# A two-layer GELU block on one core: both layers in 64-row halves of the matmul array, with another start and another end

## The chip, the core and the metric

The kernel runs on one core of a Trainium2 chip. The metric is the device time of one execution in microseconds, the median of several runs. A profile gives the same execution's span, from its first instruction to its last, and what each engine did in it: TensorE (PE, with its weight loads as PEld), VectorE (DVE), ScalarE (ACT), GpSimd (POOL) and SyncE (SP, which here only issues transfers).

## The reference

```python
# x: 1 x 2048 x 448, w1: 448 x 1792, w2: 1792 x 448, all bf16
def reference(x, w1, b1, w2, b2):
    h = jnp.einsum("bsd,df->bsf", x, w1) + b1
    h = jax.nn.gelu(h, approximate=True)
    return jnp.einsum("bsf,fd->bsd", h, w2) + b2
```

The inner size of layer 1 is 448 = 3 x 128 + 64, so three and a half times the 128 rows of the matmul array. That of layer 2 is 1792 = 14 x 128.

## The kernel before

The 2048 tokens are worked on in four blocks of 512 (`c`). Within a block the 14 tiles of 128 features come in four groups of 4, 4, 4 and 2. For each group layer 1 is done (features on the partitions, 512 tokens as columns), then its GELU, then the group's share of layer 2 (tokens on the partitions, 448 columns), which adds up in four PSUM banks `acc` over the groups. The first block's x is turned on TensorE at the start; the other three are turned by transfers (`transpose=True`).

The start: four tiles of 128 tokens, each turned in four blocks of 128 features. The fourth holds the last 64 features twice, so that both halves of the array can read them.

```python
warm(NWARM)                                     # 5 matmuls of 512 columns on ones
for t in range(STC):
    pr.op("vector", ... xr[:, t, :] <- xn[:, t, D3:D] twice ..., event=("xr", t))
    for k in range(KT + 1):                     # KT = 3
        src = xn[:, t, k * P:(k + 1) * P] if k < KT else xr[:, t, :]
        pr.op("tensor", ... e.transpose(stage(t)[...], src, ident), ...)
    eng = "scalar" if t in (1, 3) else "vector"
    pr.op(eng, evac, after=[("xt", t)], event=("xT0", t))     # 128 x 512 from PSUM
    # [b1 is turned here for t == 1]
warm(NFILL)                                     # 2 more
```

Layer 1 of a group: first the last 64 rows of the inner size, two feature tiles at a time in the two halves of the array, then three matmuls of 128 rows for each tile. Line numbers of the profile stand beside them.

```python
for j in range(n):
    for lo in (0, 1):
        rows = slice(lo * H, (lo + 1) * H)      # H = 64
        pr.op("tensor", ... e.matmul(bank[ft], lhsT=w1r[rows, 2 * gi + j, :],
              rhs=xT[rows, KT, c0:c1], start=True, stop=False))              # L205
for ft in fts:
    for k in range(KT):
        pr.op("tensor", ... e.matmul(bank[ft], lhsT=w1_sb[:, k, ft * P:(ft + 1) * P],
              rhs=xT[:, k, c0:c1], start=False, stop=k == KT - 1))           # L211
    pr.op("scalar", ... GELU of bank[ft] into g, bias b1 ...)                # L216
```

Layer 2, for each feature tile of the group and each of the four token tiles; after the last feature tile VectorE adds b2, and SyncE stores:

```python
pr.op("tensor", ... e.matmul(acc[st][:, 0:D], lhsT=g[:, ft, j * P:(j + 1) * P],
      rhs=w2_sb[:, ft, :], start=ft == 0, stop=fin))                         # L229
if fin:
    pr.op("vector", ... out_sb = acc[st] + b2_bc ...)                        # L233
    pr.dma("sync", ... out <- out_sb[:, j, :] ...)
```

The first group of the first block is done in two halves of 256 tokens. In the last block layer 2 of the last groups is ordered so that the four token tiles end one after the other.

Of the kernel before, what the change touches and what calls it, by code (L numbers as in the profile page):

```python
# [8 lines left out]
FP32 = mybir.dt.float32  # L9


class Program:

# [5 lines left out]
    def __init__(self, nc, es):  # L21
        self.nc, self.es = nc, es
        self.lists = {e: [] for e in self.COMPUTE + ("sync",)}
        self.sems = {e: es.enter_context(nc.semaphore(f"sem_{e}")) for e in self.COMPUTE}
        self.count = dict.fromkeys(self.COMPUTE, 0)
        self.where = {}

    def op(self, engine, make, after=(), event=None):
        if event is not None:
            self.count[engine] += 1  # L30
            self.where[event] = (f"sem_{engine}", self.sems[engine], self.count[engine])
        self.lists[engine].append((make, tuple(after), self.sems[engine] if event else None, 1))

    def dma(self, engine, make, event, after=()):
        if event not in self.where:
            name = "dma_" + "_".join(str(p) for p in (event if isinstance(event, tuple) else (event,)))
            self.where[event] = (name, self.es.enter_context(self.nc.semaphore(name)), 0)
        name, sem, n = self.where[event]
        self.where[event] = (name, sem, n + 16)
        self.lists[engine].append((make, tuple(after), sem, 16))  # L40

    def barrier(self, engine, after):
        self.lists[engine].append((None, tuple(after), None, 0))

    def emit(self, block):
        for name in self.lists:
            getattr(block, name)(lambda eng, name=name: self._run(eng, name))

    def _run(self, eng, name):
        seen = {}  # L50
        for make, after, sem, inc in self.lists[name]:
            for event in after:
                key, s, value = self.where[event]
                if seen.get(key, 0) < value:
                    eng.wait_ge(s, value)
                    seen[key] = value
            if make is None:
                continue
            done = make(eng)
            if sem is not None:  # L60
                done.then_inc(sem, inc)


def bass_standalone__dense_activation_gelu__prompt_kernel(
# [10 lines left out]
    P = 128  # L75
    H = P // 2
    SC = 512
    assert B == 1 and S % SC == 0 and F == 14 * P and D == 3 * P + H
    x2, out2 = x[0], out[0]
    NSC, NST, STC, NFT = S // SC, S // P, SC // P, F // P  # L80
    KT = 3
    D3 = KT * P
    GROUPS = [(0, 1, 2, 3), (4, 5, 6, 7), (8, 9, 10, 11), (12, 13)]
    GC = 4 * P
    NWARM = 5
    NFILL = 2

    with ExitStack() as es:
        sb = lambda name, shape, dt: es.enter_context(nc.sbuf_tensor(name, shape, dt))
        xT = sb("xT", [P, KT + 1, S], BF16)  # L90
        w1_sb = sb("w1_sb", [P, KT, F], BF16)
        w1r = sb("w1r", [P, NFT // 2, P], BF16)
        w2_sb = sb("w2_sb", [P, NFT, D], BF16)
        xn = sb("xn", [P, STC, D], BF16)
        xr = sb("xr", [P, STC, P], BF16)
        ident = sb("ident", [P, P], BF16)
        junk = sb("junk", [P, 1], BF16)
        b1n = sb("b1n", [NFT, P], BF16)
        b1_f = sb("b1_f", [P, NFT], FP32)
        b2_bc = sb("b2_bc", [P, D], BF16)  # L100
        g = sb("g", [P, NFT, S], BF16)
        out_sb = sb("out_sb", [P, NST, D], BF16)
        ps = [es.enter_context(nc.psum_tensor(f"ps_{i}", [P, SC], FP32)) for i in range(4)]
        acc = [es.enter_context(nc.psum_tensor(f"acc_{i}", [P, SC], FP32)) for i in range(4)]

# [4 lines left out]

        x0v = x2[0:SC, :].rearrange("(p t) d -> p t d", t=STC)
        o0v = out2[0:SC, :].rearrange("(p t) d -> p t d", t=STC)

        def group_of(ft):
            return min(ft // 4, len(GROUPS) - 1)


        for a in (0, 2):
            pr.dma("sync", lambda e, a=a: e.dma_start(xn[:, a:a + 2, :], x0v[:, a:a + 2, :]), ("x", a))
        pr.dma("scalar", lambda e: e.dma_start(b1n[:, :], b1.rearrange("(c p) -> c p", p=P)), "b1n")  # L120

        def load_w1(k):
            c0, c1 = k * GC, min((k + 1) * GC, F)
            pr.dma("sync", lambda e: e.dma_start(
                w1_sb[:, :, c0:c1], w1[0:D3, c0:c1].rearrange("(k p) f -> p k f", p=P)), ("w1", k))
            half = (c1 - c0) // 2
            for lo in (0, 1):
                pr.dma("sync", lambda e, lo=lo: e.dma_start(
                    w1r[lo * H:(lo + 1) * H, 2 * k:2 * k + half // P, :],
                    w1[D3:D, c0 + lo * half:c0 + (lo + 1) * half].rearrange("d (j q) -> d j q", q=P)), ("w1", k))  # L130

        def load_w2(k):
            a, b = GROUPS[k][0], GROUPS[k][-1] + 1
            pr.dma("sync", lambda e: e.dma_start(
                w2_sb[:, a:b, :], w2[a * P:b * P, :].rearrange("(f p) d -> p f d", p=P)), ("w2", k))

        for k in range(len(GROUPS)):
            load_w1(k)
            load_w2(k)
        pr.dma("sync", lambda e: e.dma_start(b2_bc[:, :], b2.partition_broadcast(P)), "b2")  # L140
        for c in range(1, NSC):
            for slot, d0 in enumerate((0, P, 2 * P, D - P)):
                pr.dma("sync", lambda e, c=c, slot=slot, d0=d0: e.dma_start(
                    xT[:, slot, c * SC:(c + 1) * SC], x2[c * SC:(c + 1) * SC, d0:d0 + P], transpose=True), ("xT", c))
# [6 lines left out]
        pr.op("scalar", lambda e: e.activation(junk[:, :], one, ACT.Gelu_apprx_tanh))  # L151

        def warm(n):
            for _ in range(n):
                pr.op("tensor", lambda e: e.matmul(ps[1][:, :], lhsT=ones_w, rhs=ones_m, start=True, stop=True))  # L155

        def stage(t):
            return acc[t][:, 0:2 * P].bitcast(BF16)

        warm(NWARM)  # L160
        for t in range(STC):
            a = t - t % 2
            pr.op("vector", lambda e, t=t: e.tensor_copy(  # L163
                xr[:, t, :].rearrange("p (two h) -> p two h", two=2),
                xn[:, t, D3:D].unsqueeze(1).broadcast_to([P, 2, H])), after=[("x", a)], event=("xr", t))
            for k in range(KT + 1):
                src = xn[:, t, k * P:(k + 1) * P] if k < KT else xr[:, t, :]
                need = ["ident", ("x", a)] if k < KT else [("xr", t)]
                pr.op("tensor", lambda e, t=t, k=k, src=src: e.transpose(  # L169
                    stage(t)[:, k * P:(k + 1) * P], src, ident[:, :]),  # L170
                    after=need, event=("xt", t) if k == KT else None)
            eng = "scalar" if t in (1, 3) else "vector"

            def evac(e, t=t, eng=eng):
                o = xT[:, :, t * P:(t + 1) * P]
                i = stage(t).rearrange("p (k s) -> p k s", k=KT + 1)
                return e.copy(o, i) if eng == "scalar" else e.tensor_copy(o, i)  # L177

            pr.op(eng, evac, after=[("xt", t)], event=("xT0", t))
            if t == 1:  # L180
                pr.op("tensor", lambda e: e.matmul(  # L181
                    ps[3][:, 0:NFT], lhsT=b1n[:, :], rhs=ident[0:NFT, 0:NFT], start=True, stop=True),
                    after=["b1n"], event="b1T")
                pr.op("scalar", lambda e: e.copy(b1_f[:, :], ps[3][:, 0:NFT]), after=["b1T"], event="b1")
        warm(NFILL)


        owner = {3: "b1"}

        def layer1(c, gi, cols, last_cols, first_cols):  # L190
            fts = GROUPS[gi]
            n = len(fts) // 2
            c0, c1 = cols
            need = [("w1", gi)] if c == 0 else [("xT", c), ("xTd", c)]
            if c == 0:
                need += [("xT0", t) for t in range(c0 // P, c1 // P)]
            bank = {ft: ps[i] for i, ft in enumerate(fts)}
            for j in range(n):
                for lo in (0, 1):
                    ft = fts[j + lo * n]  # L200
                    rows = slice(lo * H, (lo + 1) * H)
                    after = list(need)
                    if first_cols and fts.index(ft) in owner:
                        after.append(owner[fts.index(ft)])
                    pr.op("tensor", lambda e, ft=ft, rows=rows, j=j: e.matmul(  # L205
                        bank[ft][:, c0 % SC:(c1 - 1) % SC + 1], lhsT=w1r[rows, 2 * gi + j, :],
                        rhs=xT[rows, KT, c0:c1], start=True, stop=False), after=after)
            for ft in fts:
                for k in range(KT):
                    fin = k == KT - 1  # L210
                    pr.op("tensor", lambda e, ft=ft, k=k, fin=fin: e.matmul(  # L211
                        bank[ft][:, c0 % SC:(c1 - 1) % SC + 1], lhsT=w1_sb[:, k, ft * P:(ft + 1) * P],
# [85 lines left out]
```

## Time and profile before

| | |
|---|---|
| time, median of 3 runs | 102.3 us |
| lowest and highest | 100.4 and 102.47 us |
| span of the profile | 101.4 us |
| TensorE busy | 96.2 us, 488 matmuls |
| ScalarE busy | 39.4 us |
| VectorE busy | 11.4 us |
| moved by transfers | 7.27 MB |
| first layer-1 matmul | 7.48 us |

A row of the page's groups reads: line, engine, operation, result <- operands, rows x columns of the array for TensorE, shape, count, then busy time and mean length of one, then how long the engine stood idle just before them and what ended that. The length of one matmul is its whole passage, fill and drain included; since several are under way at once, the pace is seen from when they start. The chain of work that ended last lists, in order of time, what released what, back from the last instruction: start, length and piece.

### The profile page before, as it was taken

How to read it: one execution, taken by the hardware profiler on the slowest of the kernel's cores; microseconds unless marked ns; L12 is line 12 of the kernel's file. 1: busy time of each engine (PE TensorE's matmuls, PEld its weight loads, DVE VectorE, ACT ScalarE, POOL GpSimd, SP SyncE). 2: the span in 40 equal slices, each digit the busy share in tenths (PEclk: the TensorE clock that was granted, in tenths of full speed). 3: DMA queues.
4: the chain of work that ended last, by engine and by line, in shares of the span. 5: the costliest groups of instructions: out<-in, count | busy, mean ns of one | idle time of the engine just before them, and what ended most of it. 6: DMA issues, size and time to landing. Idle time of an engine off the chain costs nothing.

```text
span 101.4 us, 1157 instructions
## 1 busy us (share of the span) xinstructions
PE 96.2 (95%) x488; PEld 42.7 (42%) x488; DVE 11.4 (11%) x25; ACT 39.4 (39%) x61; POOL 0.7 (1%) x6
## 2 busy tenths in 40 slices
PE   6689999999999999999999999999999999999990
PEld 2345553434533443534433444534433534533530
DVE  0320000100006300000008100000008000000081
ACT  4140362807231814609050906419052707238300
POOL 2000000000000000000000000000000000000000
DMA  2999989854430500000001400000002200000023
GB/s 64 275 321 333 343 187 150 75 108 92 95 79 4 177 0 0 6 0 0 0 0 48 133 0 0 0 6 3 0 0 91 91 0 0 0 0 6 0 71 110
DMA packets 13393, 7.27 MB, mean 72 GB/s; under 512 B 7244, under 2 KB 13388, under 8 KB 13388
## 3 DMA queue, kind: packets, MB, share of 16 engines
q1 hardware_dynamic: 13360, 7.20, 27.5%
q8 instruction: 4, 0.07, 0.2%
q14 instruction: 1, 0.01, 0.0%
q10 hardware_dynamic: 28, 0.00, 0.0%
HBM read 3.79 MB, written 1.84 MB: 55 GB/s over the span
## 4 chain that ended last, share of the span: by engine, by line
PE 90%; DMA 3%; ACT 2%; DVE 2%; issue 1%
PE acc L229 42%; PE ps L211 37%; PE ps L205 8%; DMA xn<-in_x_dram 3%; ACT g L216 2%; PE acc L169 2%; PE ps L155 1%; DVE xT L177 1%; DVE out_sb L233 1%; DVE xr L163 0%; PE ps L181 0%
## 5 line engine op out<-in xcount | busy, mean ns | idle before, releaser
L216 ACT ACTIVATE g<-ps,b_f 128x512 bf16<-128x512 f32 x56 | 36.7, 688 | 50.8 <-PE ps L211 50.8
L229 PE MATMUL acc<-w_sb,g 128*128 128x448 bf16 x224 | 44.9, 353 | 0.4
L211 PE MATMUL ps<-xT,w_sb 128*128 128x512 bf16 (+1 forms) x180 | 40.6, 376 | 0.0
L229 PEld LDWEIGHTS acc<-w_sb,g 128*128 128x128 bf16 x224 | 21.6, 98 | 22.3 <-ACT g L216 2.3
L211 PEld LDWEIGHTS ps<-xT,w_sb 128*128 128x128 bf16 x180 | 16.8, 101 | 22.0 <-issue 6.4
L233 DVE TENSOR_TENSOR out_sb<-acc,b_bc 128x448 bf16<-128x448 f32 x16 | 9.2, 618 | 69.4 <-PE acc L229 69.0
L205 PE MATMUL ps<-xT,w1r 64*128 64x512 bf16 (+1 forms) x60 | 9.4, 385 | 0.0
L205 PEld LDWEIGHTS ps<-xT,w1r 64*128 64x128 bf16 x60 | 1.9, 95 | 6.9 <-issue 6.9
L155 PE MATMUL ps<-const-bfloat16-1.0 128*128 128x512 bf16 x7 | 3.4, 627 | 0.8 <-PEq L283 0.8
L177 ACT COPY xT<-acc 128x512 bf16<-128x512 bf16 x2 | 1.2, 586 | 3.2 <-PE acc L169 3.2
L254 DVE COPY xT<-xT 64x512 bf16<-64x512 bf16 x3 | 0.9, 289 | 13.5 <-DMA xT<-in_x_dram 13.4
L169 PE MATMUL acc<-ident,xn 128*128 128x128 bf16 x12 | 1.8, 308 | 0.6 <-DMA xn<-in_x_dram 0.6
L151 ACT ACT_TABLE_LOAD x1 | 1.3, 1283 | 1.4 <-PEq L283 1.4
L169 PEld LDWEIGHTS acc<-ident,xn 128*128 128x128 bf16 x12 | 1.2, 136 | 1.5 <-issue 1.4
L169 PE MATMUL acc<-ident,xr 128*128 128x128 bf16 x4 | 1.2, 302 | 0.6 <-DVE xr L163 0.6
L155 PEld LDWEIGHTS ps<-const-bfloat16-1.0 128*128 128x128 bf16 x7 | 0.8, 133 | 1.6 <-issue 1.6
L163 DVE COPY xr<-xn 128x128 bf16<-128x128 bf16 x4 | 0.7, 188 | 3.5 <-DMA xn<-in_x_dram 3.5
L177 DVE COPY xT<-acc 128x512 bf16<-128x512 bf16 x2 | 0.8, 424 | 1.5 <-PE acc L169 1.5
L169 PEld LDWEIGHTS acc<-ident,xr 128*128 128x128 bf16 x4 | 0.5, 128 | 1.1 <-DVE xr L163 1.1
L148 POOL TENSOR_SCALAR_AFFINE_SELECT ident<-ident 128x128 bf16<-128x128 bf16 x1 | 0.3, 294 | 0.2 <-POOL ident L147 0.2
L151 ACT ACTIVATE junk<-const-bfloat16-1.0 128x1 bf16<-128x1 bf16 x1 | 0.2, 205 | 0.0
L147 POOL MEMSET ident<- 128x128 bf16 x1 | 0.2, 205 | 0.3 <-POOLq L283 0.3
(7 smaller groups left out, 0.9 us busy)
## 6 DMA issues: line engine op xcount, KB each, us to landing
out_dram<-out_sb SPq DMA_DIRECT2D x16, 112.0 KB, 1.7
w_sb<-in_w_dram SPq DMA_DIRECT2D x3, 448.0 KB, 6.1
w_sb<-in_w_dram SPq DMA_DIRECT2D x3, 384.0 KB, 4.2
xn<-in_x_dram SPq DMA_DIRECT2D x2, 224.0 KB, 2.8
w_sb<-in_w_dram SPq DMA_DIRECT2D x1, 224.0 KB, 4.6
w1r<-in_w_dram SPq DMA_DIRECT2D x6, 32.0 KB, 4.3
w_sb<-in_w_dram SPq DMA_DIRECT2D x1, 192.0 KB, 4.5
xT<-in_x_dram SPq DMA_TRANSPOSE x12, 3.6
```

The lines of the kernel that those rows point to most:

```text
L148: pr.op("gpsimd", lambda e: e.affine_select(out=ident[:, :], in_=ident[:, :], compare_op=ALU.not_equal, fill=1.0, base=0, pattern=[[-1, P] ...
L151: pr.op("scalar", lambda e: e.activation(junk[:, :], one, ACT.Gelu_apprx_tanh))
L155: pr.op("tensor", lambda e: e.matmul(ps[1][:, :], lhsT=ones_w, rhs=ones_m, start=True, stop=True))
L163: pr.op("vector", lambda e, t=t: e.tensor_copy(xr[:, t, :].rearrange("p (two h) -> p two h", two=2), xn[:, t, D3:D].unsqueeze(1).broadcast ...
L169: pr.op("tensor", lambda e, t=t, k=k, src=src: e.transpose(stage(t)[:, k * P:(k + 1) * P], src, ident[:, :]), after=need, event=("xt", t) ...
L177: return e.copy(o, i) if eng == "scalar" else e.tensor_copy(o, i)
L205: pr.op("tensor", lambda e, ft=ft, rows=rows, j=j: e.matmul(bank[ft][:, c0 % SC:(c1 - 1) % SC + 1], lhsT=w1r[rows, 2 * gi + j, :], rhs=xT[ ...
L211: pr.op("tensor", lambda e, ft=ft, k=k, fin=fin: e.matmul(bank[ft][:, c0 % SC:(c1 - 1) % SC + 1], lhsT=w1_sb[:, k, ft * P:(ft + 1) * P], r ...
L216: pr.op("scalar", lambda e, ft=ft: e.activation(g[:, ft, c * SC:(c + 1) * SC], bank[ft][:, :], ACT.Gelu_apprx_tanh, bias=b1_f[:, ft:ft + 1 ...
L229: pr.op("tensor", lambda e: e.matmul(acc[st][:, 0:D], lhsT=g[:, ft, j * P:(j + 1) * P], rhs=w2_sb[:, ft, :], start=ft == 0, stop=fin), aft ...
L233: pr.op("vector", lambda e: e.tensor_tensor(out=out_sb[:, j, :], in0=acc[st][:, 0:D], in1=b2_bc[:, :], op=ALU.add), after=[("y", c, st), " ...
L254: pr.op("vector", lambda e, cs=cs: e.tensor_copy(xT[0:H, KT, cs], xT[H:P, KT, cs]), after=[("xT", c + 1)], event=("xTd", c + 1))
```

## The change

What it does:

- **Layer 1 and layer 2 wholly in 64-row halves.** Every matmul of 128 rows becomes two of 64 rows, "a" and "b". Two tiles share a unit of two PSUM banks: in part "a" the first tile uses the upper half of the array and the second the lower, in part "b" the other way round. So the two halves always work on different banks at the same time, and the array is never switched between 128-row and 64-row tiles. Between "a" and "b" of one unit lies other work, and a wait on TensorE's own semaphore keeps both halves from one bank.
- **Order.** Layer 1 of all 14 feature tiles of a block comes first (part "a" of a pair, then part "b" of the pair before), then layer 2 of the block, two token tiles to a unit. The grouping by four goes.
- **The start.** x of the first block comes in one load. SyncE's other loads wait until GpSimd has filled a buffer `b2_z` with zeros; only the first two parts of w1 are issued earlier, on ScalarE's queue. x is turned in halves of 64 tokens side by side: the transposes of rows 0 to 63 and 64 to 127 go to two banks. VectorE moves the result as 32-bit words. Layer 1 begins with the first 256 tokens. The last 64 features are turned later, behind the first matmuls. b1 is turned on VectorE. Seven and a half warming matmuls instead of five, and none after the transposes.
- **The end.** In the last block the last two token tiles are finished side by side in two steps of columns: 0 to 319 in one unit and 320 to 447 in another. b2 is brought into the second tile's bank by one matmul of ones with `b2_z` (zeros, and b2 in rows 0 and 64), so that ScalarE can copy that tile out while VectorE adds b2 to the first. The two parts are stored by two transfers, on SyncE and ScalarE.

The diff, cut to its core:

```diff
-        for a in (0, 2):
-            pr.dma("sync", ... xn[:, a:a + 2, :] <- x0v[:, a:a + 2, :] ..., ("x", a))
+        pr.dma("sync", lambda e: e.dma_start(xn[:, :, :], x0v), "x")
+        pr.barrier("sync", ["b2z0"])
+        load_w1r(0)
+        load_w1(2)
+        ...                                   # the rest of w1, w2, b2
+        pr.op("gpsimd", lambda e: e.memset(b2_z[:, :], 0.0), event="b2z0")
+        ...
+        pr.op("scalar", lambda e: e.activation(junk[:, :], one, ACT.Gelu_apprx_tanh), event="table")
+        load_w1(0, "scalar")
+        load_w1(1, "scalar")
+        class Layer1:
+            def step(self, part, k, t0=0, t1=SC):
+                for lo in (0, 1):
+                    ft = 2 * j + lo
+                    half = lo if part == "a" else 1 - lo
+                    rows = slice(half * H, (half + 1) * H)
+                    if k < KT:
+                        lhsT = w1_sb[rows, k, ft * P:(ft + 1) * P]
+                    else:
+                        lhsT = w1r[rows, ft * P:(ft + 1) * P]
+                    ...
+                    mm(u, lo, half, slice(t0, t1), lhsT, xT[rows, k, s0 + t0:s0 + t1], ...)
+        class Layer2:
+            def part(self, name, fts):
+                for ft in fts:
+                    for lo in (0, 1):
+                        half = lo if name == "a" else 1 - lo
+                        rows = slice(half * H, (half + 1) * H)
+                        mm(u, lo, half, slice(0, self.d1 - self.d0), g[rows, ft, j * P:(j + 1) * P],
+                           w2_sb[rows, ft, self.d0:self.d1], ...)
         warm(NWARM)                           # 5 -> 7
+        warm(1, HC)
+        turn_first()
+        L[0].a(0, HC)
+        L[0].step("a", 0, HC, SC)
+        L[0].step("a", 1, HC, SC)
+        turn_rest()
+        L[0].step("a", 2, HC, SC)
+        ...
+                items[0].a()
+                for j in range(1, NPAIR):
+                    items[j].a()
+                    items[j - 1].b()
+                items[-1].b()
+        ...
+            if c + 1 < NSC:
+                for part in (head, tail):     # features 0 to 9, then 10 to 13
+                    p.part("a", part)
+                    q.part("a", part)
+                p.part("b", every)
+                q.part("b", every)
+            else:
+                q, r = Layer2(c, 2, 0, DL), Layer2(c, 2, DL, D)      # DL = 320
+                p.part("a", every)
+                q.bias(1)
+                r.bias(0)
+                q.part("a", every)
+                p.part("b", every)
+                r.part("a", every)
+                q.part("b", every)
+                r.part("b", every)
```

## The prediction

> **What bounds the kernel now.** I read the page's busy lines first, then the costliest groups, then the chain that ended last, and then TensorE alone in order of time. The page's part 1 and two rows of its part 5:
>
> ```profile
> PE 96.2 (95%) x488; PEld 42.7 (42%) x488; DVE 11.4 (11%) x25; ACT 39.4 (39%) x61; POOL 0.7 (1%) x6
> ...
> L216 ACT ACTIVATE g<-ps,b_f 128x512 bf16<-128x512 f32 x56 | 36.7, 688 | 50.8 <-PE ps L211 50.8
> L229 PE MATMUL acc<-w_sb,g 128*128 128x448 bf16 x224 | 44.9, 353 | 0.4
> ```
>
> TensorE is never really idle and ScalarE waits for it (50.8 us), so what counts is how fast matmuls follow each other. The 353 ns of one matmul is not that pace, as matmuls overlap. The pace comes from the starts. TensorE alone, in order of time, in the first block of 512 tokens, after its start (columns: start, us, engine, line, what):
>
> ```profile
> 22.04 0.61 PE L205 MATMUL ps<-xT,w1r 64*128 64x512 bf16 x4
> 22.57 2.76 PE L211 MATMUL ps<-xT,w_sb 128*128 128x512 bf16 x12
> 25.18 3.19 PE L229 MATMUL acc<-w_sb,g 128*128 128x448 bf16 x16
> 28.30 0.39 PE L205 MATMUL ps<-xT,w1r 64*128 64x512 bf16 x2
> 28.62 1.47 PE L211 MATMUL ps<-xT,w_sb 128*128 128x512 bf16 x6
> 30.22 1.69 PE L229 MATMUL acc<-w_sb,g 128*128 128x448 bf16 x8
> 31.84 0.39 PE L205 MATMUL ps<-xT,w1r 64*128 64x512 bf16 x2
> ```
>
> In the chain, a run of sixteen 448-column matmuls takes 3.03 us, so 189 ns each; by columns a 512-column one is 216 ns (189 x 512 / 448). Now compare starts. From 22.04 to 22.57 two pairs of 64-row matmuls pass: 0.53 us, where 2 x 0.216 would be 0.43. From 22.57 to 25.18 twelve full ones: 2.61 against 2.59. From 25.18 to 28.30 sixteen: 3.12 against 3.03. So about 0.10 us is lost each time the array goes from 128-row to 64-row tiles and again on the way back: 0.2 us a group. In the two-tile group, six matmuls last from 28.62 to 30.22: 1.60 against 1.30. That 0.3 is a wait for the GELU, which the chain shows in the same place:
>
> ```profile
> 28.36 0.32 PE ps L205 x2
> 28.69 0.77 PE ps L211 x3
> 29.45 0.02 issue
> 29.48 0.70 ACT g L216
> 30.18 0.05 issue
> 30.22 1.69 PE acc L229 x8
> ```
>
> The third part is the start. The same view, TensorE in order of time, near the beginning:
>
> ```profile
> 7.48 0.61 PE L205 MATMUL ps<-xT,w1r 64*128 64x256 bf16 x4
> ...
> 8.02 2.74 PE L211 MATMUL ps<-xT,w_sb 128*128 128x256 bf16 x12
> ...
> 11.23 1.59 PE L211 MATMUL ps<-xT,w_sb 128*128 128x256 bf16 x12
> ```
>
> The same twelve matmuls of 256 columns take 2.74 us first and 1.59 us three microseconds later: until about 11.4 us the array works at half pace. Of the 3.9 us from 7.5 to 11.4 half, 1.9 us, is lost.
>
> **The sum of before.** A block of 512 tokens needs 14 x 3.5 = 49 matmuls of 216 ns (10.58 us) and 56 of 189 ns (10.60), four blocks 84.7 us. To this: first layer-1 matmul at 7.5; 17 groups (the first is done in two halves of columns) x 0.2 = 3.4; three GELU waits x 0.3 = 0.9; half pace 1.9. Together 98.4; the chain has TensorE's end at 98.59. The books close, so I change them term by term. Behind the last matmul stand 0.62 us of VectorE and a store, up to 101.4.
>
> **What the Trainium skill says.** "TensorEngine Tiling (Array Packing)", Key Properties: changing the tiling mode drains the array, while tiles of one mode run in parallel. The trace agrees on both: 0.10 us a change, and two pairs of 64-row matmuls in 0.53 us, where four one after the other would need 0.86. "TensorE: Matmul & The Clock Gate", Part 1: the clock starts at half rate and is released after about 3.4 us of sustained work, in a window that does not start with the kernel. The trace agrees: half pace to 11.4 us, 3.9 us after the first layer-1 matmul; the five warming matmuls, from 0.78 to about 3 us, did not suffice. As the window's phase is by chance, it may be what spreads the three times from 100.4 to 102.47; no view here shows that. The same page, Back-to-back issue gap, gives about 81 ns for each matmul of 128 columns in a stream with weight loads, more than 128 / 2.4 = 53 ns. The trace has no such stream at full pace, but its 128-row weight loads take 98 ns each (layer 2, part 5), which points the same way.
>
> **The change, part by part.**
>
> *All layer matmuls in 64-row halves.* Each 128-row matmul becomes two of 64 rows in different halves of the array and of different banks, so 105 full matmuls a block become 105 pairs. If a pair takes what a full one takes, the work is unchanged, and no mode changes are left among them: -3.4 us. The pairs in the trace start within 0.01 us of each other and the extra over 0.43 is explained by the change of mode, so I take the pace as the same, with 2 ns a pair of doubt: 420 x 2 ns = +0.8.
>
> *Layer 2 behind the whole of layer 1.* Per pair of feature tiles TensorE needs 7 x 0.216 = 1.51 us and ScalarE two GELUs, about 0.66 apiece by the timeline (four in 2.63 us), so 1.3: ScalarE keeps up. Its last two end some 1.6 us after layer 1, and layer 2 needs them only after ten tiles of one pair of outputs and ten of the other (20 x 0.189 = 3.8 us; in the last block after 12 x 0.189 = 2.3). The three GELU waits go: -0.9.
>
> *The start.* x comes as one load of 448 KB and most weights are held back until GpSimd has written its zeros. Before, the two halves of x were there at about 3.5 and 4.0 (issued at 0.75 and 1.20, 2.8 us to landing). I put the whole at 4.0. Then come 24 half transposes, twelve pairs at the 107 ns that the old ones took at half pace, 1.3 us, and they no longer wait for the fourth block of each tile: before, two waits for VectorE and two filler matmuls carried the start to 7.5. First layer-1 matmul at 5.6: -1.9. Two more transpose pairs inside layer 1 and the two bias matmuls at the end: +0.4.
>
> *Half pace.* Warming now lasts 7 x 0.427 + 0.213 = 3.2 us, to about 4.0, straight up to the transposes. With good phase the array is at full pace when layer 1 begins (loss 0); with a bad one it is 3 to 4 us later (loss 1.5 to 2). I take 0.9: -1.0.
>
> *The last two tiles side by side.* Their 448 columns are split into 320 and 128. 28 pairs of 320 cost 135 ns each, as by columns. 28 pairs of 128 columns should cost 54, but I expect the weight loads or the issue of four instructions to hold them near 105 (an estimate, from the 98 ns load): 28 x (135 + 105 - 189) = +1.4. What it buys: the last reading of PSUM is 128 columns on VectorE beside 128 on ScalarE, which need no b2 because it was added by a matmul. I estimate 0.25 us instead of 0.62, then one small store. After TensorE's end 2.4 us instead of 2.8.
>
> *The sum.* TensorE ends at 5.6 + 84.7 + 0.4 + 0.8 + 0.9 + 1.4 = 93.8; with 2.4 the span is 96.2. The profile of before (101.4) lies 0.9 under the median of its times, and half of that I carry over: 96.6 us.
>
> **Rivals.** *The issue becomes the bound.* Instructions double: two loads and two matmuls in 189 ns, 47 ns each. Suppose one needed 58 ns: a pair would take 232: over four blocks, 196 pairs lose 16 ns and 224 lose 43, 12.8 us together, and the kernel would take some 109. For it speaks that nothing in this trace sustains such a rate for long; against it, twelve 256-column matmuls with their loads ran in 1.59 us with the first one or two still at half pace, near 109 ns for two instructions, and both loads of a pair begin together. One in twelve.
>
> *The start waits elsewhere.* The first two weight loads are issued on ScalarE's queue behind its table load of 1.3 us; if they land only at 7 us, or the 24 drains and copies come late, layer 1 begins at 7.5 as before: 98.5 us. Against it: ScalarE's earlier issue took only 0.6 us, and 192 KB is little beside what moved from 2 to 4 us (near 290 GB/s).
>
> *The narrow last step costs more.* At 150 ns a pair it adds another 1.3 us, all on the path: 97.9.
>
> *Everything goes well:* full pace from the first layer-1 matmul and a pair at exactly 216 and 189 ns: 94.7.
>
> **Range and chances.** 96.6 us, eight in ten between 94.4 and 99.3. Faster by over 2% means under 100.25; only the first rival, or two of the others together, miss it. Faster 0.90, within 2% 0.05, slower 0.05.
>
> **What would show it.** Right: TensorE's starts in a middle block give 10.6 us for layer 1 and 10.6 for layer 2 with no gap between; first layer-1 matmul before 6 us; matmuls of 256 columns at 109 ns early on; the 28 pairs of 128 columns in about 3 us; no GELU in the chain. Wrong: a middle block clearly over 21.6 us, idle TensorE before layer 1 ended by a load, or a chain that runs through ScalarE.

## The result, and the profile after

The changed kernel takes 93.66 us (median of 6 runs, 93.50 to 93.91). The kernel before, beside it, takes 102.06 us (100.4 to 102.47). The ratio is 0.9285 with a 95% interval from 0.9214 to 0.9357; like the column "fast" in the table of experiments, it leaves out executions over 1.5% above the fastest of the same kernel. The spans of the two profiles are 101.4 and 92.6 us: 8.8 us to explain.

The chain that ended last, by start, length and piece, is the whole kernel in eight pieces:

```profile
0.74 0.04 issue
0.78 3.36 PE u L197 x8
4.14 0.75 PE u L349 x24
4.89 1.10 PE u L222 x8
6.00 0.09 PE u L349 x2
6.09 84.39 PE u L222 x702
90.48 0.02 issue
90.50 0.27 ACT out_sb L330
```

There is no GELU and no transfer in it. From the warming matmuls (L197) over the transposes (L349) to the last layer matmul, TensorE releases itself. L222 is the one line that issues the matmuls of both layers, and `u` are the units of two PSUM banks. What follows the last piece is the landing of one store.

TensorE alone, in order of time, through layer 2 of the second block (start, us, engine, line, what):

```profile
36.27 0.81 PE L222 MATMUL u<-xT,w_sb 64*128 64x512 bf16 x6
36.92 0.38 PE L222 MATMUL u<-xT,w1r 64*128 64x512 bf16 x2
37.13 10.75 PE L222 MATMUL u<-w_sb,g 64*128 64x448 bf16 x112
47.73 0.59 PE L222 MATMUL u<-xT,w_sb 64*128 64x512 bf16 x4
```

Three pairs of 512 columns last from 36.27 to 36.92 (0.65, so 216 ns a pair), 56 pairs of 448 from 37.13 to 47.73 (10.60, so 189 ns). The 0.10 us at each change between row lengths, seen before, is gone; so is the gap ahead of layer 2. A middle block runs from 26.56 to 47.73, 21.17 us, where the kernel before took 22.32. Its beginning here, and then the same two places in the chain of before (54.23 - 31.91):

```profile
26.56 2.10 PE L222 MATMUL u<-xT,w_sb 64*128 64x512 bf16 x18
```

```profile
31.91 0.54 PE ps L205 x4
...
54.23 0.54 PE ps L205 x4
```

The difference of 1.15 us is eight changes of row length at 0.106 (measured below) and one GELU wait of 0.30.

The start, same view:

```profile
4.07 0.82 PE L349 MATMUL u<-ident,xn 64*128 64x64 bf16 x24
4.75 1.25 PE L222 MATMUL u<-xT,w_sb 64*128 64x256 bf16 x10
5.79 0.29 PE L349 MATMUL u<-ident,xr 64*128 64x64 bf16 x4
5.92 0.93 PE L222 MATMUL u<-xT,w_sb 64*128 64x256 bf16 x8
```

Layer 1 begins at 4.75 us instead of 7.48. Its first five pairs of 256 columns take 1.04 us, 208 ns each, still half pace; the pair at 5.92 is followed within 0.12 us by the next.

The end, as stretches of time with the busy time and number of instructions of each engine in them (us, PE, PEld, DVE, ACT, POOL, then clock and transfers):

```profile
79.47:82.12 2.65, 2.65 (x32) 1.32 (x28) 0.00 (x0) 1.76 (x4) 0.00 (x0) 1.00 0.00 0
82.17:84.07 1.90, 1.90 (x32) 1.90 (x30) 0.00 (x0) 0.00 (x0) 0.00 (x0) 1.00 0.00 0
89.41:90.21 0.80, 0.80 (x31) 0.80 (x27) 0.49 (x1) 0.43 (x1) 0.00 (x0) 1.00 0.03 7
```

These are 14 pairs of 448 columns (189 ns a pair), 14 of 320 (136) and, in the last line, the last 14 of 128, all but the final start. The last 14 need only about 57 ns a pair: 27 weight loads pass in 0.80 us, though one is 94 ns long by the page's groups, so three are under way at a time.

```profile
L222 PEld LDWEIGHTS u<-w_sb,g 64*128 64x128 bf16 x504 | 25.0, 94 | 17.8
```

### The profile page after: what moved, and what is told of

It is laid out like the page before. It is cut to its first block, busy times and chain, and to the rows that moved or that the text cites. A ratio compares the mean times of both kernels' runs of the same rounds, so it can differ in the third digit from the quotient of the medians.

```text
span 92.6 us, 2057 instructions
## 1 busy us (share of the span) xinstructions
PE 89.6 (97%) x940; PEld 45.7 (49%) x940; DVE 13.9 (15%) x37; ACT 38.2 (41%) x63; POOL 1.7 (2%) x8
## 4 chain that ended last, share of the span: by engine, by line
PE 97%; ACT 0%; issue 0%
PE u L222 92%; PE u L197 4%; PE u L349 1%; ACT out_sb L330 0%
## 5 line engine op out<-in xcount | busy, mean ns | idle before, releaser
L280 ACT ACTIVATE g<-u,b_f 128x512 bf16<-128x512 f32 x56 | 34.9, 685 | 39.5 <-PE u L222 39.5
L222 PE MATMUL u<-w_sb,g 64*128 64x448 bf16 (+2 forms) x504 | 43.2, 329 | 0.0
L222 PE MATMUL u<-xT,w_sb 64*128 64x512 bf16 (+1 forms) x342 | 41.2, 377 | 0.0
L222 PEld LDWEIGHTS u<-w_sb,g 64*128 64x128 bf16 x504 | 25.0, 94 | 17.8
L222 PEld LDWEIGHTS u<-xT,w_sb 64*128 64x128 bf16 x342 | 16.0, 94 | 20.1 <-DVE xT L362 0.2
L333 DVE TENSOR_TENSOR out_sb<-u,b_bc 128x448 bf16<-128x448 f32 (+2 forms) x16 | 8.9, 590 | 62.9 <-PE u L222 62.9
L222 PE MATMUL u<-xT,w1r 64*128 64x512 bf16 x56 | 10.4, 376 | 0.0
L222 PEld LDWEIGHTS u<-xT,w1r 64*128 64x128 bf16 x56 | 2.6, 94 | 3.4
L197 PE MATMUL u<-const-bfloat16-1.0 128*128 128x512 bf16 (+1 forms) x8 | 3.4, 598 | 0.8 <-PEq L486 0.8
L197 PEld LDWEIGHTS u<-const-bfloat16-1.0 128*128 128x128 bf16 x8 | 1.0, 136 | 2.4 <-issue 2.4
L362 DVE TENSOR_SCALAR xT<-u 128x128 uint32<-128x128 uint32 (+1 forms) x7 | 1.8, 286 | 0.8 <-PE u L349 0.8
L349 PEld LDWEIGHTS u<-ident,xn 64*128 64x128 bf16 x24 | 0.7, 125 | 0.6 <-DMA xn<-in_x_dram 0.6
L349 PE MATMUL u<-ident,xn 64*128 64x64 bf16 x24 | 0.8, 237 | 0.0
```

Source lines behind the costliest of these rows:

```text
L197: pr.op("tensor", lambda e: e.matmul(unit[0][:, 0, 0:cols], lhsT=ones_w, rhs=ones_m[:, 0:cols], start=True, stop=True))
L222: o = pr.op("tensor", lambda e: e.matmul(unit[u][:, lo, cols], lhsT=lhsT, rhs=rhs, start=start, stop=stop, skip_group_check=skip), after=a ...
L280: pr.op("scalar", lambda e, lo=lo, ft=ft: e.activation(g[:, ft, c * SC:(c + 1) * SC], unit[u][:, lo, :], ACT.Gelu_apprx_tanh, bias=b1_f[:, ...
L333: pr.op("vector", lambda e, j=j, lo=lo: e.tensor_tensor(out=out_sb[:, j, d0:d1], in0=unit[u][:, lo, 0:d1 - d0], in1=b2_bc[:, d0:d1], op=AL ...
L349: pr.op("tensor", lambda e, half=half, rows=rows: e.transpose(o(half), i(rows), ident[rows, rows]), after=after + ["ident"], event=event i ...
L362: pr.op(engine, lambda e: e.tensor_single_scalar(out(U32), in_(U32), 0, ALU.bitwise_or), after=after, event=event)
```

## The experiments

All medians in us, with the lowest and highest run; the span is that of the profile.

| run | what differs | median | fast | runs | span |
|---|---|---|---|---|---|
| changed kernel | | 93.66 | 93.66 | 93.50-93.91 | 92.6 |
| after_again | nothing | 93.70 | 93.70 | 93.35-94.16 | 92.3 |
| full_l2 | layer 2 in 128 rows | 95.03 | 95.03 | 94.31-95.22 | 93.6 |
| full_both | both layers in 128 rows | 99.34 | 99.34 | 98.61-99.43 | 98.0 |
| end_plain | last block like the others | 94.52 | 94.52 | 94.22-94.93 | 92.8 |
| last_64 | split at 384 instead of 320 | 94.09 | 94.09 | 93.69-94.64 | 92.4 |
| warm_two | 2 1/2 warming matmuls, not 7 1/2 | 95.41 | 95.35 | 94.23-95.89 | 94.2 |
| no_hold | loads not held back | 96.40 | 95.20 | 95.11-98.83 | 94.1 |
| no_hold_first | not held, w1's second part in front | 93.69 | 93.69 | 93.43-94.32 | 92.2 |
| x_two | x in two loads, one queue | 95.66 | 94.81 | 94.19-96.13 | 94.8 |
| x_act | x in two loads, two queues | 94.42 | 94.40 | 93.58-95.92 | 94.6 |
| b_warm | kernel before, gaps filled | 100.50 | 100.50 | 100.40-100.76 | 98.9 |
| b_order | kernel before, layer 1 ahead of layer 2 | 101.29 | 101.29 | 100.70-101.94 | 100.1 |

### Are the changes of tiling the cost, or do halves flow better?

The theory: what the halves save is only the drain at each change. The rival: they have a worth of their own. Both runs undo halves and keep the order, the start and the end. The first puts layer 2 back in full rows (part "a" does all, part "b" nothing):

```diff
-                for ft in fts:
+                for ft in fts if name == "a" else ():
                     for lo in (0, 1):
...
-                        mm(u, lo, half, ..., g[rows, ft, j * P:(j + 1) * P], w2_sb[rows, ft, ...], ...)
+                        mm_full(u, lo, ..., g[:, ft, j * P:(j + 1) * P], w2_sb[:, ft, ...], ...)
```

> The changed kernel with layer 2 back in 128-row matmuls, all else kept. Theory (each change of the array's tiling costs 0.1 us, the halves have no worth of their own): 9 changes come back (in and out of layer 2 in each block, two more for the bias matmuls), so +0.9 us: 94.5 us; 128-row matmuls again 216 and 189 ns apart. Rival (the halves make matmuls flow better, because one half's weights load beside the other's work): layer 2 slower in itself, +2 us or more. The same run tells of the narrow last step: 56 matmuls of 128 columns in full rows. If weight loads bind without the halves, they stand near 98 ns apart and cost another +1.2 us (95.7); if not, 56 ns.

Measured: 95.03 us; the span grows by 1.04. TensorE alone around layer 2 of the same block:

```profile
37.26 0.38 PE L222 MATMUL u<-xT,w1r 64*128 64x512 bf16 x2
37.57 10.77 PE L228 MATMUL u<-w_sb,g 128*128 128x448 bf16 x56
48.27 0.60 PE L222 MATMUL u<-xT,w_sb 64*128 64x512 bf16 x4
```

The last pair of layer 1 takes 0.31 where a pair takes 0.216, and the 56 matmuls 10.70 where 56 x 0.189 is 10.60. Each change costs 0.10 and a matmul of full rows keeps its 189 ns: no sign of the rival. The narrow step in full rows (28 matmuls of 128 columns) has its first start at 89.79 us and its last at 91.29: 27 steps of 56 ns. So weight loads do not bind at 128 columns with or without halves.

The second run also puts layer 1 in full rows; only its last 64 inner rows stay in halves:

```diff
+                if part == "b" and k < KT:
+                    return
                 for lo in (0, 1):
...
-                    rows = slice(half * H, (half + 1) * H)
+                    rows = slice(half * H, (half + 1) * H) if k == KT else slice(0, P)
...
```

> Both layers back in 128-row matmuls, only the last 64 inner rows of layer 1 in halves; order, start and end of the changed kernel kept. Theory: 51 changes of tiling at 0.1 us come back, +5.1 us: 98.8 us, and with the run before (9 changes) a straight line. Rival (it is the order or the start that gained, not the changes of tiling): under 96 us.

Measured: 99.34 us, span +5.4 us. TensorE alone within layer 1:

```profile
30.67 0.39 PE L222 MATMUL u<-xT,w1r 64*128 64x512 bf16 x2
30.99 1.47 PE L228 MATMUL u<-xT,w_sb 128*128 128x512 bf16 x6
32.40 0.39 PE L222 MATMUL u<-xT,w1r 64*128 64x512 bf16 x2
```

0.32 for the pair instead of 0.216 and 1.41 for six instead of 1.30. With 9 changes the span is 1.04 longer, with 51 it is 5.4: 0.12 and 0.106 us a change. A middle block, which no start reaches, is cleaner: from the first layer-1 matmul to that of the next block it takes 21.17 us in the changed kernel, 21.38 in full_l2 (26.89 to 48.27, 2 changes) and 22.44 in full_both (28.20 to 50.65, 12 changes). That is 0.106 us a change in both. It also tells that the order of the work alone does not need the halves, but that without them it would cost more changes (51) than the kernel before had (34).

### What is the GELU wait worth?

The kernel before, with its last block's order in every block:

```diff
-                last = c == NSC - 1
+                last = True
```

> The kernel before, with the order of its last block in all four blocks: layer 1 of the two-tile group comes before layer 2 of the group of four, so that layer 2 does not follow at once on the two-tile group's GELU. Theory: the three waits of 0.3 us go and nothing else changes, -0.9 us, 101.2; in the trace the six matmuls of the two-tile group are followed by layer 2 without a gap. Rival (the wait only moves, for the order makes PSUM banks come free later): 102, with a gap in another place.

Measured: 101.29 us. In the third block, TensorE alone:

```profile
46.94 0.39 PE L205 MATMUL ps<-xT,w1r 64*128 64x512 bf16 x2
47.26 1.47 PE L211 MATMUL ps<-xT,w_sb 128*128 128x512 bf16 x5
48.57 4.70 PE L229 MATMUL acc<-w_sb,g 128*128 128x448 bf16 x24
```

From 47.26 to 48.57 are 1.31 us for six matmuls (one is missing from the records), where 1.60 stood before. From the first layer-2 matmul to the end of the span, which leaves the start out, the kernel before takes 88.70 us (12.65 to 101.35) and this run 87.77 (12.31 to 100.08): 0.93 less, so the wait has not moved elsewhere. The times alone do not show it: they stand against 101.77 us for the kernel before, counted as in the column "fast", with a ratio of 0.9998 and an interval from 0.9942 to 1.0054. They also hold the start, whose length varies from run to run.

### What ends the half pace?

First the kernel before, with nothing but TensorE's gaps filled:

```diff
-    NWARM = 5
+    NWARM = 6
...
             pr.op(eng, evac, after=[("xt", t)], event=("xT0", t))
+            if t in (0, 2):
+                warm(1)
```

> The kernel before with one change: six warming matmuls instead of five, and one more behind the transposes of the first and of the third tile, so that TensorE works nearly without a gap from 0.8 us. Theory (the half pace of before came from its idle gaps): full pace begins before layer 1 or soon after, -1 to -1.9 us: 100.2 to 101, and a smaller spread than the 2.07 us of before. Rival (the transposes, whatever fills their gaps, put the release off): 102, the same spread.

Measured: 100.50 us, and 102.26 for the kernel before beside it. TensorE alone at the first layer-1 group:

```profile
7.12 1.48 PE L213 MATMUL ps<-xT,w_sb 128*128 128x256 bf16 x12
8.53 0.39 PE L207 MATMUL ps<-xT,w1r 64*128 64x256 bf16 x4
```

The twelve matmuls that took 2.74 us now take 1.48, and layer 1 begins at 6.79 instead of 7.48. Three added matmuls on ones, which compute nothing of the result, take 1.76 us off the kernel, and its runs lie within 0.36 us of each other where those of the kernel before lay within 1.34. So it was not the transposes as such that kept the array at half pace, but what filled, or did not fill, the time between them. Whether the idle time counts or the small share of ordinary matmuls, this run does not separate.

Then the changed kernel with less warming (`NWARM` from 7 to 2):

> The changed kernel with two and a half warming matmuls instead of seven and a half, so that TensorE stands idle from about 1.9 us until x is there. Theory (steady work from the start is what ends the half pace by 5.9 us, in windows whose phase is by chance): the half pace lasts until 8 to 11 us, +1.3 to +2.5 us, 95 to 96.2, and the runs spread by over 1 us, as those of the kernel before do. Rival (the half pace ends at a fixed time or only by layer matmuls): 93.7, the same spread of 0.4 us.

Measured: 95.41 us, runs over 1.66 us. The same 20 matmuls (one pair of 256 columns, nine of 512), first in the unaltered kernel run again, then here:

```profile
5.64 2.23 PE L222 MATMUL u<-xT,w_sb 64*128 64x256 bf16 x20
```

```profile
6.18 3.52 PE L222 MATMUL u<-xT,w_sb 64*128 64x256 bf16 x20
```

1.29 us more, which is six pairs of 512 columns at half pace: it lasts to about 8.8 us. The theory holds in this; that the windows' phase is by chance is not tested by it. x also landed later in this profile (4.25 us; 3.73 to 4.08 in the others with the same loads), which the theory did not foresee and nothing here explains.

### What do the held-back loads protect?

The wait of SyncE for GpSimd's zeros taken out:

```diff
         pr.dma("sync", lambda e: e.dma_start(xn[:, :, :], x0v), "x")
-        pr.barrier("sync", ["b2z0"])
         load_w1r(0)
```

> SyncE's loads no longer wait for GpSimd's zeros. Theory (the hold gives x the transfer engines alone): x lands 0.3 to 0.6 us later and everything with it, 94.0 to 94.3. Rival (x was issued first and is through before the others matter): 93.7.

Measured: 95.20 us in the column "fast", 1.5 more, where 0.3 to 0.6 was expected. x lands at 4.25 us, but so it did in warm_two with the hold, and at 4.03 in no_hold_first without it, so the delay of x that the theory has is not shown. TensorE alone:

```profile
6.30 0.41 PE L221 MATMUL u<-xT,w_sb 64*128 64x256 bf16 x2
7.51 2.12 PE L221 MATMUL u<-xT,w_sb 64*128 64x512 bf16 x18 [0.80 <-DMA w_sb<-in_w_dram]
```

It stands still until the second part of w1 has landed (7.46 us, though issued at 1.29). The next run aims at that alone: the part goes in front of SyncE's other loads, and so from ScalarE's queue to SyncE's, still without the wait.

```diff
-        pr.barrier("sync", ["b2z0"])
+        load_w1(1)
         load_w1r(0)
...
-        load_w1(1, "scalar")
```

> SyncE's loads again not held back, but the second part of w1 is issued by SyncE right behind x, ahead of the others. In the run without the hold TensorE stood still from 6.3 to 7.5 us until that part had landed (7.46 us, issued at 1.29 on ScalarE's queue). Theory (the hold protects that part from loads that overtake it): with it in front it lands by 5.5 us, the standstill goes, 93.8 to 94.3. Rival (without the hold the transfers as a whole are too crowded): a standstill of 0.5 us or more stays, 94.8 or more.

Measured: 93.69 us; TensorE does not stop:

```profile
5.55 2.23 PE L221 MATMUL u<-xT,w_sb 64*128 64x256 bf16 x20
```

So what the hold protects is the second part of w1. Holding the late loads back is one way; issuing the needed part in front is another, with the same time (93.70 for the unaltered kernel beside it). Since the part changed its place and its queue together, the two are not separated.

### Can x be there sooner?

x in two loads on SyncE's queue, transposes after each, one warming matmul less:

```diff
-    NWARM = 7
+    NWARM = 6
...
-        pr.dma("sync", lambda e: e.dma_start(xn[:, :, :], x0v), "x")
+        for h in (0, 1):
+            pr.dma("sync", ... xn[:, 2 * h:2 * h + 2, :] <- x0v[:, 2 * h:2 * h + 2, :] ..., ("x", h))
...
```

> x of the first block in two loads of 256 tokens, one warming matmul less. Theory: the first half is there at about 3.5 instead of 3.9 us, its transposes start 0.4 earlier, the second half's follow at 4.1; layer 1 begins some 0.25 us earlier, half of which counts while the pace is half: 93.4 to 93.6. Rival: the second load lands later than the single one did, and the time is the same or up to 0.2 us longer.

Measured: 94.81 us in the column "fast", a miss by over 1 for both; the rival has the late second load right. TensorE alone, in the profile, which is of the longest execution (96.13 us):

```profile
3.65 0.50 PE L350 MATMUL u<-ident,xn 64*128 64x64 bf16 x12
4.91 0.50 PE L350 MATMUL u<-ident,xn 64*128 64x64 bf16 x12 [0.76 <-DMA xn<-in_x_dram]
```

The first half came early (3.48 us), the second (4.86 us) a full microsecond later than the single load. The standstill between them costs twice: layer 1 begins at 5.45, and the 20 matmuls that were compared for warm_two take 3.73 us, so half pace lasts to about 9.7 us. Then both halves at once, on two queues, the weights behind them, and the short last warming matmul left out:

```diff
-        pr.dma("sync", lambda e: e.dma_start(xn[:, :, :], x0v), "x")
+        for h, engine in enumerate(("sync", "scalar")):
+            pr.dma(engine, ... xn[:, 2 * h:2 * h + 2, :] <- x0v[:, 2 * h:2 * h + 2, :] ..., ("x", h))
+        load_w1(0)
...
-        load_w1(0, "scalar")
...
-        warm(1, HC)
```

> x of the first block in two loads at once, one on SyncE's and one on ScalarE's queue, the first two parts of w1 behind them, and the last short warming matmul left out. Theory (x's second half was late in the earlier try because a weight load lay ahead of it): both halves land by 3.8 us, transposes begin near 3.85, layer 1 near 4.55 instead of 4.75: -0.1 to -0.2 us, 93.4 to 93.6. Rival (the transfer engines are full, order alone doesn't matter): x lands at 3.9 to 4.2 as before, 93.6 to 94.

Measured: 94.42 us; the halves land at 3.96 and 4.17 us. The profile, of its longest execution, has layer 1 at 5.28 and half pace to about 9.5 us; its lowest run, 93.58, is that of the unaltered kernel. Neither version beats the changed kernel.

It is not x that comes too late here: the transposes begin at 4.01 us, and at 4.08 in after_again. The first part of w1, now issued by SyncE behind x, lands at 5.14 us where ScalarE's queue had brought it at 4.45, and layer 1 begins 0.14 us after that. The profile puts this wait down to VectorE, whose first piece of x was ready at 4.69:

```profile
5.28 1.25 PE L223 MATMUL u<-xT,w_sb 64*128 64x256 bf16 x10 [0.45 <-DVE xT L363]
```

In six more runs layer 1 begins 0.14 us after that part of w1 has landed (full_l2, end_plain, last_64, warm_two, no_hold, no_hold_first); in end_plain the chain names it:

```profile
0.80 3.93 DMA w_sb<-in_w_dram
4.73 0.14 issue
4.87 0.76 PE u L222 x10
```

So an earlier x alone gains little: in the two profiles of the unaltered kernel this part landed only 0.19 and 0.30 us before layer 1 began. And no run tried x in two loads with no weight load issued between them, as the kernel before has it: there the halves land at 3.49 and 4.02 us.

### What does the split end bring?

The last block done like the other three (`if c + 1 < NSC:` made `if True:` for layer 2):

> The last block's layer 2 done like the other blocks': two tiles of 448 columns end together, both read by VectorE, four stores on SyncE. Theory (the split pays by a shorter reading behind the last matmul): TensorE ends 0.1 us earlier, but 2 x 0.6 us on VectorE and a store stand behind it instead of 0.3 and a store, so +0.6 us: 94.3. Rival (the split costs as much as it brings): within 0.2 us of 93.66.

Measured: 94.52 us, 0.86 more than the changed kernel. The time from the first layer-2 matmul of the last block to the end of the span does not depend on the start: 13.70 us here (79.12 to 92.82), 13.13 in the changed kernel (79.47 to 92.60). TensorE's last start is 0.34 us earlier in this count, and what stands behind it is longer, by VectorE:

```profile
89.91 1.15 DVE L333 TENSOR_TENSOR out_sb<-u,b_bc 128x448 bf16<-128x448 f32 x2 [1.49 <-PE u L222]
```

```profile
90.47 0.29 DVE L333 TENSOR_TENSOR out_sb<-u,b_bc 128x128 bf16<-128x128 f32 x1 [0.29 <-PE u L222]
```

1.15 us of reading in the plain end (first line), 0.29 in the split one. The net of 0.57 is as expected; the other 0.29 between the medians is not explained by this. Then the split at 384 (`DL = D - H`):

> The split of the last two tiles at column 384 instead of 320, so that 64 columns come last. If pairs of 64 columns run as by columns (27 ns and a little, 29), TensorE ends at the same time and the last reading is shorter by some 0.05 us: 93.6. Rival (a floor of issue or weight loads shows at 64 columns): pairs stay near 50 ns, 28 x 21 ns = +0.6 us: 94.2.

Measured: 94.09 us, 0.43 more. Both theories miss the time. There is no floor: the last 14 pairs of 64 columns take 0.45 us, 32 ns each. But the time from layer 2 to the end is 13.46 us, 0.33 longer than with the split at 320. VectorE and the two stores:

```profile
89.60 0.69 DVE L333 TENSOR_TENSOR out_sb<-u,b_bc 128x384 bf16<-128x384 f32 x2 [1.53 <-PE u L222]
...
90.20 0.38 SPq L290 DMA_DIRECT2D out_dram<-out_sb  x1
90.34 0.40 ACTq L290 DMA_DIRECT2D out_dram<-out_sb  x1
```

TensorE's last start (89.78) lies 10.80 us after the first of layer 2, against 10.74 with the split at 320. The reading behind it is shorter by about as much, so the narrow step's store is issued after 11.36 us, against 11.38. But this store, issued at 90.34, lands at 92.41, 2.07 us later, where that of the changed kernel took 1.71 (90.85 to 92.56): this is the 0.33. The two stores are now issued 0.14 us apart instead of 0.62, which may be why; no run tests it.

The changed kernel again, unaltered, measured beside no_hold_first, x_act and b_order:

> The changed kernel once more, unaltered, beside the three other runs of this call. All theories: 93.5 to 94 us; the first matmul of layer 1 near 4.75 us.

Measured: 93.70 us, layer 1 from 4.76.

## Why the prediction was right, and where it was not

It was right in direction and in what carries the gain: the changes of tiling, the GELU waits and the earlier start were found with nearly the sizes foreseen or larger ones. One mechanism that it added was not found, the weight loads as a floor of the narrow step. In size it was too careful: 96.6 us were predicted, 93.66 measured. The median lies under the low end of 94.4; the ratio 0.9285 on the 102.3 us it started from makes 95.0, inside the range. Term by term, in the order of its sum:

| step of the prediction | predicted | measured |
|---|---|---|
| changes of tiling gone | -3.4 | 34 x 0.106 = -3.6 (full_both) |
| three GELU waits gone | -0.9 | -0.93 (b_order's trace) |
| first layer-1 matmul | 5.6 us | 4.75 us |
| half pace costs | 0.9 | 0.5 (5 pairs x 0.10) |
| doubt in the pace, 2 ns a pair | +0.8 | 0 |
| extra transposes and bias matmuls | +0.4 | +0.2 |
| narrow last step | +1.4 | +0.1 |
| behind TensorE | 2.4 | 2.3 |

"Measured" for the last two: layer 2 of the last block takes 10.74 us from its first to its last start, and 56 pairs at 189 ns are 10.60; with the last start at 90.21 and one pair more, 2.33 us remain to 92.6. The terms that were off add up to 0.85 + 0.4 + 0.8 + 0.2 + 1.3 + 0.1 = 3.65 us; from 96.2, the predicted span, to 92.6 are 3.6.

*The narrow last step* is the step that failed most. "I expect the weight loads or the issue of four instructions to hold them near 105 (an estimate, from the 98 ns load)": this took the length of a load for the time between loads. At 128 columns a pair takes about 57 ns, at 64 columns 32, and loads of 94 ns overlap threefold. The page's 81 ns for a stream of 128-column matmuls, which the prediction leaned on, is not what this kernel shows: 56 ns in full rows (full_l2).

*The start* was mis-sized in the transposes. The prediction took 107 ns a pair from the old ones, which moved 128 columns each; the new ones move 64, and from the first of them to layer 1 twelve pairs took 0.68 us. x was there at 3.90, near the 4.0 assumed; over nine profiles with one load of x it was there between 3.73 and 4.26, so this was in part luck.

*The pace*: the 2 ns of doubt were not needed. A pair of halves takes what a full matmul takes, to the nanosecond shown. The first rival, an issue rate that binds, is refuted by the same pairs of 64 columns: two loads and two matmuls in 32 ns, over 14 pairs.

*Half pace*: in this profile and in the one repeated it ends between 5 and 6 us; in end_plain, last_64 and no_hold_first it is over by 4.4, before layer 1, which is the loss of 0 foreseen for a good phase. The late end foreseen for a bad one was seen only with less warming or with gaps ahead of layer 1 (8.8 to 9.7 us). The twelve runs of the unaltered kernel, from 93.35 to 94.16 us, have no room for its loss of 1.5 to 2.

*The rival "start waits elsewhere"* did not happen in the size feared (7 us), but it is nearer than the prediction put it. The first part of w1 sets the beginning of layer 1 in seven of the runs, at 4.75 to 5.28 us. And no_hold, the same start with one wait less on SyncE, loses 1.5 us, with a standstill of 0.80 us ahead of the second part. The prediction gave the held-back loads no term of their own, which cost nothing only because the kernel has the wait.

*The split end*: worth 0.57 us within the last block, of which the prediction saw the shorter reading and set against it a cost of 1.4 that does not exist.

## What to carry to other kernels

Where full and partial rows of the array alternate, count the changes: 0.106 us each here, and pairs of half-row matmuls on different banks kept the pace of full rows. Keep TensorE working without a gap from its first instruction until the real work begins: with gaps, half pace lasted to 8.8 us and more here, and three dummy matmuls took 1.8 us off the old kernel. Where work starts late, look at the landing of everything that it needs: the wait was put down to VectorE in x_act and was for a weight load. Take the pace of instructions from their starts, and not from the length of one.

## What the runs showed of the hardware

- Weight loads are no floor in a stream of short matmuls: 56 ns apart at 128 columns in full rows (full_l2), 32 ns a pair at 64 columns in halves (last_64), though one load's record is 94 to 98 ns long. "TensorE: Matmul & The Clock Gate", Back-to-back issue gap, has about 81 ns; the runs decide.
- Half pace ends between 4.0 and 6.2 us in the eight profiles in which TensorE works nearly without gaps ahead of layer 1 (the changed kernel twice, full_l2, full_both, end_plain, last_64, no_hold_first, b_warm), and between 8.8 and 11.4 us in the five with gaps there (warm_two, x_act, x_two, b_order, the kernel before). Both spreads, 2.2 and 2.6 us, would fit in the window of about 3.4 us on the same page (Part 1). That the window's phase is what spreads the runs was not tested; the narrow spread of b_warm (0.36 us) only agrees with it.
- The granted clock does not show half pace: it reads 1.00 for the kernel before from 7 to 11 us too. Only the starts of the matmuls do.
- A load issued at 1.29 us on ScalarE's queue landed at 7.46 us while SyncE issued its loads from 1.20 us on, and at 5.24 us where these were held back to 1.91. By what rule the transfers share the engines stays open.
- One load of x of 448 KB landed between 3.73 and 4.26 us in nine profiles. Two loads of 224 KB landed at 3.96 and 4.17 us on two queues, at 3.48 and 4.86 on one with a part of w1 issued on ScalarE's queue between them, and at 3.49 and 4.02 on one with no weight load between (the kernel before). Why is open.
